# A fused recurrent attention and two mixture-of-experts layers on one core: feed-forward products for two groups of tokens at once

## The chip, the cores and the metric

The kernel runs on one core of a Trainium2 chip. The metric is the time of one execution on the device in microseconds (us), the median of repeated runs. The engines are named as in the profile: PE (TensorE, matrix products and transposes), DVE (VectorE), ACT (ScalarE), POOL (GpSimd) and SP (which here issues every load and store).

## The reference, cut to what matters

```python
# 1. attention with a decaying state: 4 batches, 8 heads, 768 steps, head size 48
for t in range(S):
    cur = einsum('bhd,bhe->bhde', u * k[t], v[t])
    y[t] = einsum('bhd,bhde->bhe', r[t], state + cur)
    state = w[t][..., None] * state + einsum('bhd,bhe->bhde', k[t], v[t])
x = y as 3072 tokens x 384
# 2. feed-forward: w_in 384 x 2048, w_out 2048 x 384 (both float64)
h = x @ w_in;  g = h * cos(h);  x = g @ w_out
# 3. soft mixture of 8 experts, 4 slots each
logits = x @ phi                                   # 3072 x 32
d = softmax of logits over the tokens;  slot_input = d.T @ x
slot_out[e] = relu(slot_input[e] @ w1[e]) @ w2[e]
out = (softmax of logits over the slots) @ slot_out
```

## The kernel before, in words

The tokens go through in pieces. Attention takes **blocks** of 128 tokens, 24 of them (j = 0 to 23); the feed-forward layer takes **groups** of 256 tokens, 12 of them (g = 0 to 11). A group needs the two blocks with its tokens.

*Attention block j.* r, k, w and v are loaded and transposed by PE (L141). DVE makes the running products of the decay by two scans over 520 columns (L156 `qt`, L164 `pt`) and scales the transposed r and k with them (L187 `L`, two halves; L199 `ks`). PE multiplies them (L208 `A`), DVE puts the causal mask on (L222, two halves), PE makes the block's part of the state (L259 `U`), DVE carries the state on (L269 `z`, L277 `st_state`), PE makes y (L288, and L297 for the term with u), and ACT and DVE store x as two parts, xh and the remainder xl (L309, L313).

*Feed-forward group g.* The hidden layer of 2048 columns is cut into 8 units of 256 (i = 0 to 7). `b_h` (L448 to L464) computes a unit in two halves of 128 hidden columns. A half takes, for each of three pieces of the 384 inputs, three products into one PSUM area: high weights times xh (L462), high weights times xl (L463), low weights times xh (L464), nine products with 256 columns (the tokens of the group). A unit's 128x512 result then goes through four steps for g = h*cos(h): a whole number of turns (`b_turns`, ACT, L474), the remainder (`b_rest`, DVE, L478), the cosine (`b_cos`, ACT, L482) and the product with h (`b_mul`, DVE, L486). PE transposes g four times (`b_t`, L494) and ACT copies that to `gt` (L499). `b_l` (L507) multiplies g with `p_sb` (w_out times phi, prepared at the start) into the group's logits. After the last unit the logits go through a running softmax over the tokens (`s_sum` to `s_dc`), and `s_e_pe` (L603) adds the weighted sum of g over the group's tokens to `E`, which DVE folds into `e_sb` (L612).

*Buffers.* x for groups 3n and 3n+1 lies in `x01`, for groups 3n+2 in a tile of its own. g has four buffers, gt twelve; h has two PSUM areas (`ps_h`), the transposed g one, the logits one, and the softmax's PSUM tiles (`ps_m`) one.

*The order.* The instructions of this part, those of SP too, are issued as the string HEAD lists them: a step per word, such as `h.2.1.0` (unit 1 of group 2, first half) or `scan.7`. Each engine executes its instructions in that order. The start of HEAD also decodes w_in and w_out from float64 (`raw`, `abs`, `mx`, `d1`, `d2a`, `d2b`, `whi`, `wn`, `wc`, `oT` and others), the word `att` closes the buffers of the attention, and then the first of the 16 expert weight tiles of 1.5 MB, `we0` to `we15`, are loaded (L678, L682): NTW of them into the space of the attention, five at `we.` words, NLATE after HEAD, the rest after the first products with experts.

*The tail.* After the last group the slot inputs, the hidden layer of the experts (`hidden`, L797) and the expert outputs (`expert_out`, L838) are computed. The outputs of the experts are columns 0 to 255 (part 0) and columns 256 to 383 (part 1); `copy_so` (L884, L885) copies each with ACT and DVE, `slots_round` (L850, L851) splits it into two, and `store` (L857 to L880) multiplies with the combine weights, copies from PSUM by ACT and DVE in turn and writes to the output: tiles 0 to 11 in two parts, tiles 12 to 23 in all 384 columns at once, 16 stores in all.

Of the kernel before, what the change touches and what calls it, by code (L numbers as in the profile page):

```python
# [21 lines left out]
def rwkv_moe_kernel(ctx: ExitStack, tc: tile.TileContext, r, k, v, w, u, w_in, w_out, phi, w1, w2, cst, out):  # L22
# [18 lines left out]
    NTW = 6  # L41
    NLATE = 3
# [9 lines left out]
    b_stack = ctx.enter_context(ExitStack())  # L52
    sm_p = b_stack.enter_context(tc.tile_pool(name="sm", bufs=2, side="right"))
# [53 lines left out]
    xh_t, xl_t = {}, {}  # L107
    x2_p = []
# [485 lines left out]
    def s_e_pe(g, hf):  # L594
# [51 lines left out]
    if True:  # L646
# [51 lines left out]
        def exp_table():  # L698
# [60 lines left out]
        with tc.manual_schedule(engines=ORDERED):  # L759
# [58 lines left out]
            crt = tw_p.tile([128, NT], F32R, tag="tw", name="cr")[0:96]  # L818
            cr = crt.rearrange("p (j b t) -> p j b t", j=4, b=NB)
# [35 lines left out]
            def store(i, tag, tiles, n):  # L855

                cols = slice(0, DM) if i is None else parts[i]  # L857
                w = cols.stop - cols.start
                if tag not in obs:
                    obs[tag] = wu_p.tile([128, 3072], F32, tag=tag, name=f"ob{tag}")  # L860
                ob = obs[tag][:, n * w:(n + len(tiles)) * w].rearrange("p (t f) -> p t f", f=w)
                nb = max(1, 512 // w)
                for b0 in range(0, len(tiles), nb):
                    k = min(nb, len(tiles) - b0)
                    ps = pb(f"o{tag}{tiles[b0]}_{w}")[:, 0:k * w].rearrange("p (t f) -> p t f", f=w)
                    for t in range(k):
                        tt = tiles[b0 + t]
                        if tt < 2 and i == 0:
# [208 lines left out]
```

## Time and profile before

| quantity | value |
|---|---|
| median of three runs | 550.89 us (550.5, 550.89, 551.18) |
| the profiled execution's own time | 552.63 us |
| its span in the profile | 550.8 us |
| mean granted TensorE clock, as a share of full speed | 0.968 |
| PE busy | 507.3 us (92% of the span), 6832 instructions |
| PE weight loads busy (beside PE's products) | 437.9 us (80%) |
| DVE busy | 433.2 us (79%), 825 instructions |
| ACT busy | 315.8 us (57%) |
| POOL busy | 124.8 us (23%) |
| chain of work that ended last | PE 64%, DVE 16%, ACT 8%, DMA 5%, SP's queue 4% |

The span is from the first to the last instruction that the profiler recorded; the profiled execution took 1.83 us more than its span, and 1.74 us more than the median. Busy times are shares over the whole span, whose stages differ: decode and first blocks, attention and feed-forward side by side, the last groups alone, the experts and the output. In a timeline, the start of an instruction is recorded; the durations of PE's products overlap, since one begins before the one ahead of it has ended.

### The profile page before, as it was taken

The page shows a single profiled execution, that of the slowest core. Times are in us where ns is not written, and L with a number is a line of the kernel's source. Part 1 is how long each engine was busy: PE and PEld are TensorE (multiplying, and loading weights), DVE is VectorE, ACT ScalarE, POOL GpSimd, SP SyncE. Part 2 cuts the span into 40 slices and gives each one's busy share as a digit, 9 for nine tenths or more (in the row PEclk, how much of TensorE's full clock was granted, in tenths as well). Part 3 has the DMA queues.
Part 4 walks back from the last instruction along what each step waited for, and adds up shares of the span by engine and source line. Part 5 has one row for each costly group of instructions (what it writes and reads, how often), then busy time and mean ns, then how long its engine had stood idle before and what let it go on. Part 6 is the DMA issues. An engine that isn't in the chain of part 4 may idle for free.

```text
span 550.8 us, 16214 instructions
## 1 busy us (share of the span) xinstructions
PE 507.3 (92%) x6832; PEld 437.9 (80%) x6832; DVE 433.2 (79%) x825; ACT 315.8 (57%) x663; POOL 124.8 (23%) x163
## 2 busy tenths in 40 slices
PE   2759879989999999999999999999999999997994
PEld 1537668879898898998988989999899899874564
DVE  4989998997888879987878898989788777563413
ACT  3246567746757465576555765656566856655422
POOL 4520120254044122321320410623124000001300
PEclk9977998999999999999999999999999999997996
DMA  8994756444432523411441243173131692477937
GB/s 195 252 247 102 177 121 182 122 75 74 73 60 44 87 50 65 74 27 28 71 72 30 52 81 56 22 126 48 20 57 30 231 377 82 175 266 275 401 116 262
DMA packets 144360, 67.52 MB, mean 123 GB/s; under 512 B 127520, under 2 KB 131616, under 8 KB 144288
## 3 DMA queue, kind: packets, MB, share of 16 engines
q1 hardware_dynamic: 144288, 66.49, 47.8%
q8 instruction: 54, 0.88, 0.7%
q14 instruction: 18, 0.15, 0.1%
HBM read 61.75 MB, written 4.72 MB: 121 GB/s over the span
## 4 chain that ended last, share of the span: by engine, by line
PE 64%; DVE 16%; ACT 8%; DMA 5%; SPq 4%; issue 2%; ACTq 0%; DVEq 0%
PE h L462 9%; PE h L464 9%; PE h L463 9%; PE gT L494 6%; PE E L603 4%; PE l L507 3%; PE y L288 3%; PE A L208 3%; PE U L259 2%; PE so L838 2%; DMA rawi<-in_moe_w_in_dram 2%; PE hps L797 2%; DVE g L478 2%; DVE L L222 2%; ACT g L482 2%
## 5 line engine op out<-in xcount | busy, mean ns | idle before, releaser
L462 PE MATMUL h<-x,wu 128*128 128x256 f32 x573 | 171.8, 300 | 1.3 <-DVE g L486 1.3
L464 PE MATMUL h<-x,wu 128*128 128x256 f32 x573 | 161.0, 281 | 0.0
L463 PE MATMUL h<-x,wu 128*128 128x256 f32 x573 | 161.0, 281 | 0.0
L462 PEld LDWEIGHTS h<-x,wu 128*128 128x128 f32 x573 | 108.9, 190 | 3.5 <-DVE g L486 1.7
L463 PEld LDWEIGHTS h<-x,wu 128*128 128x128 f32 x573 | 109.1, 190 | 0.2
L464 PEld LDWEIGHTS h<-x,wu 128*128 128x128 f32 x573 | 108.7, 190 | 0.0
L482 ACT ACTIVATE g<-g,half_pi 128x512 f32<-128x512 f32 (+1 forms) x97 | 69.4, 719 | 42.6 <-DVE g L478 41.6
L486 DVE TENSOR_TENSOR g<-g,h 128x512 f32<-128x512 f32 x96 | 64.9, 678 | 27.8 <-ACT g L482 27.2
L474 ACT ACTIVATE g<-h 128x512 int32<-128x512 f32 x96 | 57.0, 596 | 40.0 <-PE h L464 33.0
L478 DVE SCALAR_TENSOR_TENSOR g<-g,h 128x512 f32<-128x512 int32 x96 | 65.0, 678 | 17.0 <-ACT g L474 15.8
L251 POOL TENSOR_TENSOR bv<-vz,bo 64x384 f32<-64x384 f32 x48 | 43.8, 912 | 140.5 <-DVE bo L243 54.4
L499 ACT COPY gt<-gT 128x512 f32<-128x512 f32 x92 | 53.4, 584 | 31.2 <-PE gT L494 30.6
L494 PE MATMUL gT<-cs,g 128*128 128x128 f32 x384 | 58.6, 277 | 0.2
L494 PEld LDWEIGHTS gT<-cs,g 128*128 128x128 f32 x384 | 44.1, 141 | 6.0 <-issue 3.3
L169 POOL TENSOR_TENSOR ru<-rn,u_b 128x384 f32<-128x384 f32 x24 | 26.8, 1118 | 58.5 <-issue 19.5
L193 POOL MEMSET L<- 64x512 f32 x32 | 16.7, 521 | 95.9 <-PE y L288 81.5
L156 DVE TENSOR_TENSOR_SCAN qt<-wf,one_b 128x520 f32<-128x520 f32 x24 | 31.1, 1297 | 7.3 <-ACT wf L151 7.3
L222 DVE TENSOR_TENSOR L<-A,cs 64x512 f32<-64x512 f32 x48 | 33.1, 689 | 3.5 <-PE A L208 2.4
L274 ACT COPY rzs<-z 64x192 f32<-64x192 f32 x96 | 33.4, 348 | 3.6 <-DVE z L269 2.6
L187 DVE TENSOR_TENSOR L<-rT,pt 64x512 f32<-64x512 f32 x48 | 32.9, 686 | 1.6 <-PE rT L141 0.6
L164 DVE TENSOR_TENSOR_SCAN pt<-wf,ini_f 128x520 f32<-128x520 f32 x24 | 31.7, 1321 | 0.1
L288 PEld LDWEIGHTS y<-L,rzs 128*32 128x32 f32 x1536 | 25.0, 112 | 6.6 <-ACT rzs L274 2.3
(176 smaller groups left out, 845.4 us busy)
## 6 DMA issues: line engine op xcount, KB each, us to landing
we<-in_moe_w_dram SPq DMA_DIRECT2D x16, 1536.0 KB, 10.4
rawi<-in_moe_w_in_dram SPq DMA_DIRECT2D x7, 768.0 KB, 5.5
wn<-in_w_dram SPq DMA_DIRECT2D x24, 192.0 KB, 4.0
kn<-in_k_dram SPq DMA_DIRECT2D x24, 192.0 KB, 3.8
rn<-in_r_dram SPq DMA_DIRECT2D x24, 192.0 KB, 4.0
vz<-in_v_dram SPq DMA_DIRECT2D x48, 96.0 KB, 3.1
rzs<-in_v_dram SPq DMA_DIRECT2D x96, 48.0 KB, 2.8
rawo<-in_moe_w_out_dram SPq DMA_DIRECT2D x2, 1536.0 KB, 8.2
```

The source lines that it names most:

```text
L222: nc.vector.tensor_tensor(out=L[h, a], in0=ps[h], in1=mask[h].unsqueeze(1).to_broadcast([64, NS, C]), op=ALU.mult)
L251: nc.gpsimd.tensor_tensor(out=bv[h], in0=vn_t[j][h, :, c, :], in1=bo[h].to_broadcast([64, H, D]), op=ALU.mult)
L288: nc.tensor.matmul(ps[m:m + 32, o, c * C:(c + 1) * C], lhsT=rz[:, c, p, a, 32 * b:32 * b + 32], rhs=L[:, a, 2 * p + c, :], start=m not in ...
L462: nc.tensor.matmul(hp, lhsT=wh, rhs=xh[:, c, :], start=(c == 0), stop=False)
L463: nc.tensor.matmul(hp, lhsT=wh, rhs=xl[:, c, :], start=False, stop=False)
L464: nc.tensor.matmul(hp, lhsT=wl, rhs=xh[:, c, :], start=False, stop=(c == KD - 1))
L474: nc.scalar.activation(gt.bitcast(I32), hp, AF.Copy, bias=0.25, scale=1.0 / TWO_PI)
L478: nc.vector.scalar_tensor_tensor(out=gt, in0=gt.bitcast(I32), scalar=-TWO_PI, in1=hp, op0=ALU.mult, op1=ALU.add)
L482: nc.scalar.activation(gt, gt, AF.Sin, bias=half_pi[:, 0:1])
L486: nc.vector.tensor_tensor(out=gt, in0=gt, in1=hp, op=ALU.mult)
L494: nc.tensor.transpose(ps[:, tt, mm, :], gt[:, mm, tt * 128:(tt + 1) * 128], ident)
L499: (nc.vector.tensor_copy if NBK * g + i >= ATT and i in (1, 2) else nc.scalar.copy)(t, pend.pop(("gT", g, i)))
```

## The change

`WIDE_G = (2, 4, 6, 8)` names the groups that begin a pair: 2 and 3, 4 and 5, 6 and 7, 8 and 9. For these eight groups `b_h2` takes the place of `b_h`: one half of 128 hidden columns for both groups of the pair, nine products with 512 columns, 16 units (i = 0 to 15) for a pair. `b_turns`, `b_rest`, `b_cos`, `b_mul`, `b_t` and `b_tc` work on tiles of the same 128x512 as before, with the second half of the tile now the second group in place of the second half of the hidden columns. x of a pair lies in one tile, `x01` for pairs 0, 4 and 8, a tile of the `x2` pool for the others. g and gt of the wide units get one and four extra buffers. `b_l` issues four products of 512 columns for four units of a pair, and the softmax chain of each group reads its half of that PSUM tile. `s_e_pe` has pieces of 128 columns for the wide groups, 32 products a group in place of 16 of 256. `bv` has one buffer in place of two. The copy of `gt` is DVE's for the last group alone. NTW goes from 6 to 5, NLATE from 3 to 4. At the end every output tile is made in part 0 and part 1 (19 stores), each part of `so` is copied by one engine, and `expert_out(1, 0)` stands ahead of the first outputs. HEAD is a list of its own from the first word on.

Cut to the functions and lines that the text speaks of:

```diff
-    NTW = 6
-    NLATE = 3
+    NTW = 5
+    NLATE = 4
+    WIDE_G = (2, 4, 6, 8)
...
-        bv = aw.tile([128, H, D], F32, tag="bv", name=f"bv{j}")
+        bv = aw.tile([128, H, D], F32, tag="bv", name=f"bv{j}", bufs=1)
...
-            x = x01[:, g % 3] if g % 3 < 2 else x2_p[0].tile([128, 2, KD, G], F32R, tag="x", name=f"x{g}")
+            if g // 2 % 2 == 0:
+                xp = x01
+            else:
+                if g % 2 == 0:
+                    x2_t.append(x2_p[0].tile([128, 2, 2, KD, G], F32R, tag="x", name=f"x{g}"))
+                xp = x2_t[-1]
+            x = xp[:, g % 2]
...
+    def b_h2(g, i):
+
+        hp = ps_h.tile([128, 2, G], F32, tag="h", name=f"h{g}_{i}")
+        h_t[g, i] = [None, None, hp]
+        o, wt, xp = (i % 4) * 128, wu[i // 4], xp_t[g]
+        for c in range(KD):
+            wh, wl = wt[:, 0, c, o:o + 128], wt[:, 1, c, o:o + 128]
+            nc.tensor.matmul(hp, lhsT=wh, rhs=xp[:, :, 0, c, :], start=(c == 0), stop=False)
+            nc.tensor.matmul(hp, lhsT=wh, rhs=xp[:, :, 1, c, :], start=False, stop=False)
+            nc.tensor.matmul(hp, lhsT=wl, rhs=xp[:, :, 0, c, :], start=False, stop=(c == KD - 1))
...
+            pool, tag = (gx_p[1], "g5") if g in WIDE_G and i % 5 == 4 else (g_p, "g")
...
+        pool, tag = (gx_p[0], "gx") if g in WIDE_G and i % 4 == 3 else (gt_p, "gt")
+        t = pool.tile([128, 2, G], F32, tag=tag, name=f"gt{g}_{i}")
+        (nc.vector.tensor_copy if g == NG - 1 and i in (1, 2) else nc.scalar.copy)(t, pend.pop(("gT", g, i)))
...
+        if g in WIDE_G:
+            if i == 3:
+                lps_t[g] = ps_l.tile([128, 512], F32, tag="l", name=f"l{g}")
+            for m in range(i - 3, i + 1):
+                nc.tensor.matmul(lps_t[g][32 * (m % 4):32 * (m % 4) + 32, :], lhsT=p_sb[:, m, :], rhs=g_t[g, m].rearrange("p m t -> p (m t)"),
+                                 start=(m < 4), stop=(m >= MF - 4))
+            return
...
+        g0 = g // 2 * 2
+        if g0 in WIDE_G:
+            for mm in range(2):
+                for tt in range(2):
+                    for q in range(4):
+                        c = hf * 256 + mm * 128
+                        nc.tensor.matmul(ps[32 * q:32 * q + 32, c:c + 128], lhsT=dt_[:, tt, :],
+                                         rhs=gt_t[g0, 8 * hf + 2 * q + mm][:, g - g0, tt * 128:(tt + 1) * 128], start=(tt == 0), stop=(tt == 1))
+            return
...
+            def outputs(i, n0, tile_=None):
+
+                cols = parts[i]
+                n = cols.stop - cols.start
+                nt = 512 // n
...
+                if tile_ is not None and n0:
+                    nc.vector.tensor_copy(ob, ps)
+                    if t1 < nt:
+                        return
+                    ob, t0 = obs[i][:, n0 % 6], 0
+                else:
+                    (nc.vector.tensor_copy if n0 % 2 else nc.scalar.copy)(ob, ps)
+                nc.sync.dma_start(out[(n0 * nt + t0) * 128:(n0 * nt + t1) * 128, cols].rearrange("(t p) f -> p t f", p=128), ob)
...
-            copy_so(0)
-            store(0, "wu0", [0], 0)
+            nc.scalar.copy(so[:, parts[0]], ops[0][:, 0:256])
+            expert_out(1, 0)
+            outputs(0, 0, 0)
             slots_out(0)
...
-lw.0 wT.0 wf.0 scan.0 z.0.0 raw.i.2 abs.i.2 mx.i.2 d1.i.2 sr.0 d2a.i.2 d2b.i.2 lk.0 kT.0 sp.0 raw.i.0.0 abs.i.0.0 mx.i.0.0 lr.0
+raw.i.0.0 abs.i.0.0 mx.i.0.0 raw.i.0.1 d1.i.0.0 abs.i.0.1 lr.0 z.0.0 d2a.i.0.0 mx.i.0.1 d1.i.0.1 d2a.i.0.1 d2b.i.0.0 d2b.i.0.1
```

Three places of the order follow. In the names, `h_4`, `g_0` and the like are feed-forward tiles by unit; the last number is an instruction's tile.

PE, in group 2, around the first half of its logits; before:

```order
L464 MATMUL h_4_2273<-x_1629,wu_698 128x256
L259 MATMUL U_2327<-vz_123,ksn_2309 64x96 x8
L288 MATMUL y_2338<-L_1942,rzs_126 32x64 x32
L507 MATMUL l_2373<-g_0_2158,p_sb 32x256 x2
L507 MATMUL l_2373<-g_1_2113,p_sb 32x256 x2
L507 MATMUL l_2373<-g_2_2299,p_sb 32x256 x2
L507 MATMUL l_2373<-g_3_2176,p_sb 32x256 x2
L494 MATMUL gT_0_2395<-cs,g_0_2158 128x128 x4
L462 MATMUL h_5_2409<-x_1629,wu_698 128x256
```

These rows end with the next half of a unit. In the change the same place has groups 2 and 3 together (L484 and L482 are products of `h`, L530 logits, L515 transposes of g, L210 `A`, L290 and L299 y, L143 and L217 transposes of the attention):

```order
L484 MATMUL h_8_2740<-x_1583,wu_691 128x512
L210 MATMUL A_2750<-L_2629,ks_2725 64x64 x16
L530 MATMUL l_2488<-g_4_2451,p_sb 32x512
L530 MATMUL l_2488<-g_5_2650,p_sb 32x512
L530 MATMUL l_2488<-g_6_2520,p_sb 32x512
L530 MATMUL l_2488<-g_7_2525,p_sb 32x512
L290 MATMUL y_2774<-L_2395,rzs_125 32x64 x32
L143 MATMUL rT_2807<-cs,rn_117 128x128 x4
L299 MATMUL y_2774<-cs,bv_2812 128x128 x3
L515 MATMUL gT_5_2836<-cs,g_5_2650 128x128 x4
L217 MATMUL kN_2843<-cs,ks_2725 128x128 x4
L482 MATMUL h_11_2848<-x_1583,wu_691 128x512
```

Before, pairs of products with 256 columns make the logits of units 0 to 3 of group 2, and the halves of units come in 256 columns; in the change four products with 512 columns make the logits of units 4 to 7 for both groups, and each product of `h` has 512 columns.

DVE, where the first instructions for group 2 stand (names with `g2_`); before:

```order
L156 SCALAR_TENSOR_TENSOR qt8_2026<-wf_127,one_b_128 128x520
L478 SCALAR_TENSOR_TENSOR g1_7_2028<-g1_7_2028,h1_7_1923 128x512
L486 TENSOR_TENSOR g1_7_2028<-g1_7_2028,h1_7_1923 128x512
L160 RECIPROCAL ini_f_129<-qt8_2026 128x8
L164 SCALAR_TENSOR_TENSOR pt8_2044<-wf_127,ini_f_129 128x520
L616 COPY e_sb_110<-E0_1971 128x512
L617 COPY st_s_113<-sg0_1786 128x1
L313 TENSOR_TENSOR x01_115<-y6_1990,x01_115 128x3x128
L222 TENSOR_TENSOR L7_1942<-A7_1945,cs_103 64x512 x2
L478 SCALAR_TENSOR_TENSOR g2_1_2113<-g2_1_2113,h2_1_2070 128x512
L486 TENSOR_TENSOR g2_1_2113<-g2_1_2113,h2_1_2070 128x512
L199 TENSOR_TENSOR ks8_2161<-kT8_2089,qt8_2026 128x512
```

Around the remainder and product of unit 1 of group 2 (L478, L486) stand scan, `L`, mask and `ks` of blocks 7 and 8. The same place in the change (there L499 is the remainder, L507 the product, L189 `L`, L224 the mask, L201 `ks`, L271 `z`, L166 `pt`):

```order
L189 TENSOR_TENSOR L8_2145<-rT8_2130,pt8_2082 64x512 x2
L507 TENSOR_TENSOR g1_7_2000<-g1_7_2000,h1_7_1981 128x512
L322 TENSOR_TENSOR x2_1583<-y7_2097,x2_1583 128x3x128
L499 SCALAR_TENSOR_TENSOR g1_6_2205<-g1_6_2205,h1_6_2068 128x512
L507 TENSOR_TENSOR g1_6_2205<-g1_6_2205,h1_6_2068 128x512
L224 TENSOR_TENSOR L8_2145<-A8_2181,cs_103 64x512 x2
L201 TENSOR_TENSOR ks9_2222<-kT9_2200,qt9_2136 128x512
L279 TENSOR_TENSOR st_state_130<-U8_2169,z8_0_2138 128x192
L271 TENSOR_TENSOR z8_1_2225<-st_state_130,qt8_1949 128x192
L499 SCALAR_TENSOR_TENSOR g2_0_2242<-g2_0_2242,h2_0_2210 128x512
L166 SCALAR_TENSOR_TENSOR pt9_2246<-wf_127,ini_f_129 128x520
L507 TENSOR_TENSOR g2_0_2242<-g2_0_2242,h2_0_2210 128x512
```

Here it is blocks 8 and 9: the attention is about one block further when group 2 begins.

SP, the loads of expert weights from the last one of `att` on; before:

```order
L678 DMA we5_6930<-in_moe2_w1_dram 128x3x1024
L678 DMA we6_7355<-in_moe2_w1_dram 128x3x1024
L682 DMA we10_7357<-in_moe2_w2_dram 128x4x768
L678 DMA we7_7406<-in_moe2_w1_dram 128x3x1024
L682 DMA we8_7408<-in_moe2_w2_dram 128x4x768
L682 DMA we9_7421<-in_moe2_w2_dram 128x4x768
L682 DMA we11_7453<-in_moe2_w2_dram 128x4x768
L682 DMA we12_7455<-in_moe2_w2_dram 128x4x768
L682 DMA we13_7457<-in_moe2_w2_dram 128x4x768
L682 DMA we14_7565<-in_moe2_w2_dram 128x4x768
L682 DMA we15_7579<-in_moe2_w2_dram 128x4x768
```

Five loads (`we11` to `we15`) stand behind `we9`. In the change, from `we4`, the last one of `att`:

```order
L717 DMA we4_6438<-in_moe2_w1_dram 128x3x1024
L717 DMA we5_6679<-in_moe2_w1_dram 128x3x1024
L717 DMA we6_6831<-in_moe2_w1_dram 128x3x1024
L721 DMA we9_6904<-in_moe2_w2_dram 128x4x768
L717 DMA we7_6918<-in_moe2_w1_dram 128x3x1024
L721 DMA we8_6920<-in_moe2_w2_dram 128x4x768
L721 DMA we10_6942<-in_moe2_w2_dram 128x4x768
L721 DMA we11_6944<-in_moe2_w2_dram 128x4x768
L721 DMA we12_6946<-in_moe2_w2_dram 128x4x768
L721 DMA we13_6948<-in_moe2_w2_dram 128x4x768
L721 DMA we14_7056<-in_moe2_w2_dram 128x4x768
L721 DMA we15_7070<-in_moe2_w2_dram 128x4x768
```

Six loads (`we10` to `we15`) stand behind `we8`; `we5` comes by a word of its own and `we9` ahead of `we7`.

## Rows read from the trace of the kernel before

**Rows 1.** The page's busy time of each engine and its chain that ended last.

```profile
PE 507.3 (92%) x6832; PEld 437.9 (80%) x6832; DVE 433.2 (79%) x825; ACT 315.8 (57%) x663; POOL 124.8 (23%) x163
...
PE 64%; DVE 16%; ACT 8%; DMA 5%; SPq 4%; issue 2%; ACTq 0%; DVEq 0%
```

**Rows 2.** Stretches: us, busy PE, PEld, DVE, ACT, POOL, then PE's clock, DMA share, GB/s.

```profile
50.00:125.00 75.00, 66.95 (x855) 55.59 (x854) 71.07 (x110) 46.13 (x92) 16.61 (x15) 0.98 0.56 130
125.00:475.00 350.00, 346.81 (x4852) 314.58 (x4852) 290.67 (x576) 216.96 (x457) 84.89 (x104) 1.00 0.35 76
```

**Rows 3.** PE's timeline along stretches of products: start us, us, engine, line.

```profile
230.68 0.60 PE L494 MATMUL gT<-cs,g 128*128 128x128 f32 x4
231.03 0.37 PE L462 MATMUL h<-x,wu 128*128 128x256 f32 x1
231.24 0.28 PE L463 MATMUL h<-x,wu 128*128 128x256 f32 x1
...
232.39 0.28 PE L463 MATMUL h<-x,wu 128*128 128x256 f32 x1
...
234.31 0.28 PE L464 MATMUL h<-x,wu 128*128 128x256 f32 x1
```

**Rows 4.** PE's timeline where products of 256 and of 512 columns stand together.

```profile
87.59 0.60 PE L404 MATMUL wl<-ai,cs 128*128 128x256 f32 x2
87.83 0.47 PE L405 MATMUL wl<-wu,neg 128*128 128x256 f32 x1
88.14 1.02 PE L404 MATMUL wl<-ai,cs 128*128 128x512 f32 x2
88.60 0.79 PE L405 MATMUL wl<-wu,neg 128*128 128x512 f32 x1
```

**Rows 5.** PE's timeline in the tail, products with 32 weight columns.

```profile
522.70 6.25 PE L838 MATMUL so<-we,wo_sb 128*32 128x256 f32 x112
...
531.16 1.08 PE L838 MATMUL so<-we,wo_sb 128*32 128x128 f32 x32
```

**Rows 6.** DVE's groups by line: count, busy us, mean ns, idle before.

```profile
L222 DVE TENSOR_TENSOR L<-A,cs 64x512 f32<-64x512 f32 x48 | 33.1, 689 | 3.5 <-PE A L208 2.4
L187 DVE TENSOR_TENSOR L<-rT,pt 64x512 f32<-64x512 f32 x48 | 32.9, 686 | 1.6 <-PE rT L141 0.6
L164 DVE TENSOR_TENSOR_SCAN pt<-wf,ini_f 128x520 f32<-128x520 f32 x24 | 31.7, 1321 | 0.1
L156 DVE TENSOR_TENSOR_SCAN qt<-wf,one_b 128x520 f32<-128x520 f32 x24 | 31.1, 1297 | 7.3 <-ACT wf L151 7.3
L269 DVE TENSOR_TENSOR z<-st_state,qt 128x192 f32<-128x192 f32 x44 | 17.8, 404 | 1.0
...
L199 DVE TENSOR_TENSOR ks<-kT,qt 128x512 f32<-128x512 f32 x24 | 16.4, 682 | 1.5 <-PE kT L141 1.1
```

**Rows 7.** PE's steps of the attention in the chain that ended last: start us, us.

```profile
234.59 1.08 PE A L208 x32
235.67 0.66 PE U L259 x16
```

**Rows 8.** What DVE waited for: us in total, times, longest us.

```profile
DVE g L486 <- ACT g L482: 27.8, 40, 1.5
DVE g L478 <- ACT g L474: 16.7, 24, 2.2
```

**Rows 9.** The stretch of the last expert loads, and SP's timeline there.

```profile
503.00:526.00 23.00, 22.88 (x374) 13.83 (x370) 9.49 (x27) 7.93 (x21) 5.87 (x9) 0.94 0.91 344
...
502.94 10.54 SPq L682 DMA_DIRECT2D we<-in_moe_w_dram  x5
```

**Rows 10.** Bytes by the page, the last stretch, and ACT's first copy of expert outputs.

```profile
HBM read 61.75 MB, written 4.72 MB: 121 GB/s over the span
...
538.50:550.80 12.30, 5.54 (x24) 5.38 (x24) 4.28 (x8) 3.23 (x7) 0.00 (x0) 0.56 0.79 275
...
529.02 0.27 ACT L884 COPY wo_sb<-so 128x128 f32<-128x128 f32 x1 [5.74 <-PE so L838]
```

More of the change, by code (lines that the diff above doesn't have):

```diff
@@ L853, in rwkv_moe_kernel @@
             obs = {}
[L855 to L868, printed above, removed]
-                            nc.tensor.matmul(ps[:, t], lhsT=cf[:, tt * 128:(tt + 1) * 128], rhs=so[:, cols], start=True, stop=True)
-                        elif i is None:
-                            o = tiles[0] * 128 + b0 + t
-                            nc.tensor.matmul(ps[:, t], lhsT=crt[:, o:o + 255:2], rhs=sr[:, cols], start=True, stop=True)
-                        else:
-                            nc.tensor.matmul(ps[:, t], lhsT=crt[:, tt * 128:(tt + 1) * 128], rhs=sr[:, cols], start=True, stop=True)
-                    pend["ob"] = 1 - pend.get("ob", 0)
-                    (nc.scalar.copy if pend["ob"] else nc.vector.tensor_copy)(ob[:, b0:b0 + k], ps)
-                t0 = tiles[0] * 128
-                dst = out[t0:t0 + len(tiles) * 128, cols]
-                nc.sync.dma_start(dst.rearrange("(p t) f -> p t f" if i is None else "(t p) f -> p t f", p=128), ob)
@@ L940 @@
-close h.1.0.0 gT.0.6 oT.12 pc.2 pT.2 oc.12 lr.6 gc.0.6 scan.6 h.1.0.1 ru.6 mul.0.7 sr.6 ps.2 bo.6 oT.14 oT.15 oc.14 l.0.5 oc.15
-om.3 kT.6 turns.1.0 rest.1.0 rz.4.0 h.1.1.0 gT.0.7 ks.6 pc.3 pT.3 ps.3 z.5.0 st.5.0 z.5.1 st.5.1 cos.1.0 mul.1.0 y.4 l.0.7 rT.6
-h.1.1.1 h.1.2.0 lw.7 ru.5 bo.5 sp.6 wT.7 h.1.2.1 L.6 lz.5 turns.1.1 rz.5.1 gc.0.7 rest.1.1 lv.6 lr.8 rz.5.0 sum.0 cos.1.1 yb.4
-xh.4 turns.1.2 xl.4 rest.1.2 wf.7 bv.5 mul.1.1 gT.1.0 cos.1.2 mul.1.2 gc.1.0 scan.7 y.5 A.6 lc.0 mask.6 h.1.3.0 h.1.3.1 turns.1.3
@@ L1024 @@
[L1024 to L1026 removed]
+            for n0 in range(6):
+                outputs(1, n0)
+HEAD = """
+raw.i.0.0 abs.i.0.0 mx.i.0.0 raw.i.0.1 d1.i.0.0 abs.i.0.1 lr.0 z.0.0 d2a.i.0.0 mx.i.0.1 d1.i.0.1 d2a.i.0.1 d2b.i.0.0 d2b.i.0.1
@@ new lines @@
+oT.12 turns.0.7 ps.2 oc.13 d2b.o.7 close oT.14 gT.0.5 oc.14 rest.0.7 oT.15 oc.15 U.5 l.0.5 oc.12 cos.0.7 om.3 scan.6 bo.5 z.5.0
+mul.0.7 rz.5.0 st.5.0 pc.3 z.5.1 A.5 mask.5 lv.6 pT.3 rz.5.1 ps.3 turns.1.1 rest.1.1 gc.0.5 sr.6 sp.6 h.1.0.0 h.1.0.1 wT.7 wf.7
+turns.1.0 cos.1.1 l.0.7 y.4 yb.4 xh.4 sum.0 rest.1.0 cos.1.0 gT.0.7 mul.1.1 scan.7 mul.1.0 kT.6 xl.4 st.5.1 ks.6 gc.0.7 h.1.3.0
+h.1.3.1 turns.1.3 rest.1.3 cos.1.3 gT.1.1 rT.6 lc.0 gc.1.1 h.1.2.0 kN.6 h.1.2.1 gT.1.0 ru.6 lr.8 turns.1.2 ksn.6 bv.5 lz.6 bo.6
@@ new lines @@
+wT.9 gT.1.3 kN.8 ksn.8 gc.1.3 cos.1.7 E.0.0 E.0.1 lz.7 mul.1.4 gT.1.4 h.1.6.0 lv.8 rz.7.0 sp.8 ru.9 zl.9 wf.9 rz.7.1 l.1.5 y.7
+rT.8 lr.10 scan.9 z.8.0 sr.9 es.0 gc.1.4 zl.8 gT.1.5 bo.9 gc.1.5 yb.7 h.1.6.1 U.8 L.8 mul.1.7 A.8 xh.7 xl.7 kT.9 turns.1.6
+rest.1.6 cos.1.6 mul.1.6 h2.2.0 mask.8 ks.9 st.8.0 z.8.1 rT.9 gT.1.7 kN.9 turns.2.0 rest.2.0 cos.2.0 sp.9 mul.2.0 lw.11 lz.8 lw.10
+h2.2.1 ksn.9 L.9 gc.1.7 rz.8.1 l.1.7 rz.8.0 sum.1 turns.2.1 lk.10 y.8 st.8.1 rest.2.1 cos.2.1 mul.2.1 wT.10 gT.1.6 wf.10 bv.8
```

267 lines of the change are left out of this document (131 added, 136 removed).

## The prediction

> **What bounds the kernel now.** I read the page's totals first, then the busy times by stretch, then PE's timeline, the waits of DVE and the chain of waits. PE is busy for 507.3 of 550.8 us and makes 64% of the chain, DVE 433.2 us and 16% [rows 1]. The totals hide two stages. From 50 to 125 us DVE is busy for 71.07 of 75 us and PE for 66.95; from 125 to 475 us PE is busy for 346.81 of 350 and DVE for 290.67 [rows 2]. So DVE sets the pace while the weights are decoded and the first blocks go through, and PE sets it in the long stage behind. A change is worth there what it takes off the bounding engine: DVE's work ahead of about 125 us, PE's work behind it, and at the end the chain from the last group to the last store.
>
> **The change part by part.** The sum is made against the profiled execution, 552.63 us (a span of 550.8 and 1.83 around it); the median of the runs is 550.89, or 1.74 lower, and I carry the difference over to it unchanged.
>
> *Products of 512 columns.* Counted in the order of PE, the feed-forward products of groups 2 to 9 go from 1152 with 256 columns to 576 with 512. The number of columns streamed is the same, so the gain is only what each instruction costs beyond its columns. In an unbroken stretch sixteen spacings, from 232.39 to 234.31 us, take 1.92 us, 0.120 each; I take 0.119, since the times are read to 0.01, so two products take 0.238 [rows 3]. The nearest products with 512 columns are those of L404: two of them take 88.60 - 88.14 = 0.46 us, 0.23 each, where two of 256 take 87.83 - 87.59 = 0.24 [rows 4]. The difference is 0.008 us, 576 x 0.008 = 4.6 us less. The trace's steps of 0.01 us leave this open: between 0 (a product of 512 takes exactly two of 256) and 7 us (0.012 each). 576 weight loads go as well; they lie beside the products in this stretch, and I give them nothing more.
>
> *Fewer starts of a stretch.* Uninterrupted stretches of `h` products go from 135 to 107 and those of logits from 38 to 28. The first product after the four transposes of g has its successor 0.21 us later (231.03 to 231.24) where 0.12 is usual [rows 3], so 38 x 0.09 = 3.4 us less. Since not each start shows this, the bounds are 1 and 5 us.
>
> *Expert sums in pieces of 128 columns.* `E` has 32 products of 128 columns for a wide group in place of 16 of 256, 128 products more in all, the columns the same. Thirty-two of 128 columns took 1.08 us and 112 of 256 took 6.25 us, or 16 in 0.89 [rows 5]; but each row includes the run-out of its last product, which weighs more in the short one. I take a third of the difference, 0.06 us a group, +0.5 in all, with 0 and 0.19 x 8 = 1.5 as bounds.
>
> *The attention runs further ahead.* The wide products need x of two groups, so four blocks where two did, and the list does their work earlier. Counted to the first remainder of group 2, DVE has 237 instructions instead of 219. In five groups of rows these are one `qt` scan more, two masks, two `L`, two `ks`, and four `z`: 1.297 + 2 x 0.689 + 2 x 0.686 + 2 x 0.682 + 4 x 0.404 = 7.0 us [rows 6]. Seven shorter ones (state, `bo`, x and a reciprocal) are estimated with `z`'s 0.404, another 2.8. In the same stretch of the list PE gets one more `A` at 1.08, two more `U` at 0.66 [rows 7] and six more transposes of four at 0.35 (from 230.68 to 231.03, [rows 3]), 4.5 us, and some y. DVE is the bound up to here [rows 2], so the stage grows by 9.8; PE, with 5 of them to do that it need not do later, gets back only that. I take +4.5 net. The bounds are 0 (DVE has gaps ahead of it: 17 and 28 us of waits for ACT in the span, [rows 8], which the extra work can fill) and 9.8 (PE does nothing in that time that helps it later).
>
> *Expert weights.* NTW falls to 5, so `we5` waits for a feed-forward buffer, and behind the last groups six loads stand in SP's queue where five did. From 503 to 526 us the DMA engines were 91% busy at 344 GB/s, with the last five loads issued from 502.94 us on [rows 9]: 23 us for five, 4.6 each. A sixth ends near 530.6 us. The eight experts' products for part 0 end near 529.0, where ACT's copy begins, and the last 16 of them take 112-fold 6.25 / 7 = 0.89 [rows 5, 10], so they begin near 528.1 and would be 2.5 us late. I take +2.4, with 0 (buffers come free earlier) and 4.6 (the whole load) as bounds. What is queued behind on SP is only the stores, which come later anyway.
>
> *Output.* Before, 12.30 us at 275 GB/s, 3.4 of the 4.72 MB written, are moved in the last stretch, from 538.5 us on [rows 10], since tiles 12 to 23 wait for part 1. In the change part 0 of all tiles, two thirds of the bytes, goes out before that; 1.6 MB stay behind part 1, 1.8 MB less, which is 6.6 us of transfer. The copies out of PSUM and their chain are as long as before (18 of 512 columns), and `so` part 0 is copied whole by ACT, where ACT took 0.27 us for its half [rows 10]; so I take a third, -2, with -4 and +2 (three more stores, one engine's longer copy) as bounds.
>
> *At nothing.* The single `bv` buffer makes POOL wait for the y term (POOL is busy for 124.8 us of the span, [rows 1] less than a quarter, so the work queued behind such a wait has room; without that room PE's y would wait for it). The copies of `gt` for group 10 go from DVE to ACT, the less busy of the two in every stretch read [rows 2]. The new beginning of the list decodes `raw.i.0` first; the same DVE instructions follow in another order, and the bound by DVE is unchanged.
>
> *Sum.* -4.6 - 3.4 + 0.5 + 4.5 + 2.4 - 2 = -2.6 us: 552.63 - 2.6 = 550.0 for a profiled execution, 550.89 - 2.6 = **548.3** for the median. Its own range is 545 to 550: the small terms against each other.
>
> **The rivals.**
> *DVE takes over in the wide stage (slower).* Two groups' remainders and products come close together, and at the first product of group 6 the list is further ahead still: two `qt` scans, two `pt` scans, eight halves of `L` and mask, one `ks`, three `z`, 2 x 1.297 + 2 x 1.321 + 8 x 0.688 + 0.682 + 3 x 0.404 = 12.6 us of DVE's work [rows 6], against some 3 us of PE's. For it: in the 350 us DVE is at 83% as it stands [rows 2], and its `L486` waits only 28 us for ACT [rows 8], so it has little room. Against it: 59 us of DVE's stage are idle. It decides if DVE is busy throughout up to group 6. Then the lead costs 12.6 - 3 = 9.6 instead of 4.5, +5.1: 553.4.
> *512 columns cost just twice 256, or nearly.* Rows 4 are only two pairs, read to 0.01 us. If the spacing were columns at the clock and a small constant, the gain of the first part shrinks. At a gain of 1.4 us the sum is +0.6, 551.5; at none +2.0, 552.9. The Trainium skill, "TensorE: Matmul & The Clock Gate", section "Back-to-back issue gap", gives for an isolated gap the columns at 2.4 GHz plus about 2.5 ns: by it 576 fewer products save 1.4 us. By it 256 columns take 0.109 us and 512 take 0.216; the rows have 0.119 and 0.23, about 0.01 more for either, so the trace supports its shape and leaves its constant open.
> *Stalls at the change of pairs (slower).* Two softmax chains now follow one another through the one `ps_m` buffer, and the logits of the last four units wait for the last `b_mul`. A wait for ACT of up to 2.2 us is in the trace [rows 8]; once a pair, 4 x 2.2 = 8.8: 557.1. Against it: the next pair's first units stand between.
> *The lead is free and the weights are on time (faster).* If the gaps of DVE take the lead, and buffers come free early, 4.5 and 2.4 go away: -9.5, 541.4. For it: 27.8 and 16.7 us of waits [rows 8]. Against it: 95% DVE in the stage where the lead is built up [rows 2].
>
> **How the numbers follow.** Forecast 0.37; DVE takes over 0.27; 512 columns no cheaper 0.13; stalls 0.08; free lead 0.15. The predicted time is the forecast's, 548.3. What a measurement of this kernel can tell from no change is about 0.2%, 1.1 us. Faster by more: most of the forecast (0.33) and the free lead (0.15), 0.48. Within it: the forecast's edge (0.04), the mild ends of the first and second rival (0.04 and 0.07), 0.15. Slower: the rest, 0.37. The range goes from 542.5, which takes in most of the way to the free lead, to 555.5, which takes in the first rival with its bounds and leaves out the stalls.
>
> **What would show it.** The spacing of two `h` products with 512 columns: 0.230 us if the first term is right, 0.238 if not. In the stretch where groups 2 and 3 are begun PE should stand idle for some 4 or 5 us, waiting for DVE, and not in groups 6 to 9; idle time of PE there by L507 or L499 of DVE would be the first rival. `so` products should wait for a DMA by about 2 us near the end, and the last store should end some 20 us after the first copy of `so`, where it was 21.8. The prediction is wrong if PE is idle at the start of each pair, or if the stage up to group 2 is not longer than before.

## The result, and the profile after

The changed kernel takes 557.22 us (median of six runs, 554.78 to 560.29) against 551.0 us: 1.0113 of the kernel before, with a 95% interval of 1.0088 to 1.0137. It is 6.2 us slower; 548.3 was forecast, and the range ended at 555.5. The profiled execution of the change is one of its fastest (555.35 us, a span of 553.4), so the two profiles differ by less than the medians do.

The page of the change, busy times and chain (against [rows 1]):

```profile
PE 503.8 (91%) x6402; PEld 404.8 (73%) x6402; DVE 435.4 (79%) x821; ACT 314.9 (57%) x663; POOL 131.0 (24%) x163
...
PE 54%; DVE 30%; ACT 7%; DMA 5%; issue 4%; SPq 0%; ACTq 0%; DVEq 0%
```

PE has 430 instructions less, but is busy for only 3.5 us less. DVE's share of the chain has gone from 16% to 30%.

The two stages again, by busy time (columns as in [rows 2]), and PE's two longest waits in the first:

```profile
50.00:125.00 75.00, 65.06 (x859) 53.78 (x858) 72.09 (x109) 49.04 (x100) 19.24 (x16) 1.00 0.52 120
125.00:475.00 350.00, 344.38 (x4375) 280.84 (x4378) 289.08 (x571) 210.49 (x446) 86.43 (x102) 1.00 0.34 64
...
PE wl L413 <- DVE L L224: 2.2, 1, 2.2
PE y L290 <- DVE L L189: 1.9, 1, 1.9
```

The longest one there before:

```profile
PE U L259 <- DMA vz<-in_v_dram: 2.4, 1, 2.4
```

PE does 1.9 us less in the first stage and 2.4 less in the second than before, so it stands idle for that much more in each; DVE is busy for 1.0 us more in the first. In the first stage two waits of PE for DVE's `L` and mask make 4.1 us; before, the longest wait there was one for a load of v.

The end is read best from PE's timeline: the sum after the last `E`, the part 0 products with expert weights, and the first output (against [rows 5, 9, 10]):

```profile
503.44 0.38 PE L805 MATMUL sum<-st_s,cs 128*128 128x1 f32 x2
...
521.74 4.52 PE L877 MATMUL so<-we,wo_sb 128*32 128x256 f32 x80
526.99 1.07 PE L877 MATMUL so<-we,wo_sb 128*32 128x256 f32 x16 [0.73 <-DMA we<-in_moe_w_dram]
531.00 2.79 PE L877 MATMUL so<-we,wo_sb 128*32 128x256 f32 x32 [2.94 <-DMA we<-in_moe_w_dram]
533.72 0.70 PE L908 MATMUL o<-wo_sb 128*128 128x256 f32 x2
...
531.00:536.00 5.00, 5.00 (x43) 3.32 (x44) 0.67 (x2) 1.48 (x4) 0.00 (x0) 0.72 0.05 18
```

The last line is a stretch of five us (columns as in [rows 2]). Before, the same sum and the first output product:

```profile
504.47 0.59 PE L765 MATMUL sum<-st_s,cs 128*128 128x1 f32 x2
...
529.66 0.70 PE L870 MATMUL owu<-wo_sb 128*128 128x256 f32 x2 [0.71 <-DVE wo_sb L885]
```

So up to the last group the change is 1.0 us ahead, and at the first output 4.1 us behind. In between, PE waits for the expert weights twice, 3.7 us in all, and runs more slowly behind the waits: the row at 531.00 has 32 products, 16 of part 0 and the first 16 of part 1, and from 531 to 536 us the granted clock is 0.72. From the first output product to the end of the span it takes 553.4 - 533.72 = 19.7 us, where it took 550.8 - 529.66 = 21.1. The 1.0 us of lead should not be built on: the profile of the kernel before is of one of its longer executions, and in `tail_new` and `before_six` below, whose order up to there is the old one, the sum began at 502.49 and 502.69, earlier than in the change.

### The profile page after: what moved, and what is told of

Read it like the earlier page. It is cut to its first block, busy times and chain, and to the rows that moved or that the text cites. A ratio compares the mean times of both kernels' runs of the same rounds, so it can differ in the third digit from the quotient of the medians.

```text
span 553.4 us, 15345 instructions
## 1 busy us (share of the span) xinstructions
PE 503.8 (91%) x6402; PEld 404.8 (73%) x6402; DVE 435.4 (79%) x821; ACT 314.9 (57%) x663; POOL 131.0 (24%) x163
## 4 chain that ended last, share of the span: by engine, by line
PE 54%; DVE 30%; ACT 7%; DMA 5%; issue 4%; SPq 0%; ACTq 0%; DVEq 0%
PE h L482 6%; PE h L484 6%; PE h L483 6%; PE gT L515 5%; DMA we<-in_moe_w_dram 3%; DVE g L499 3%; DVE g L507 3%; PE l L530 3%; DVE L L189 3%; PE A L210 3%; DVE L L224 2%; DVE pt L166 2%; PE y L290 2%; ACT g L503 2%; PE U L261 2%
## 5 line engine op out<-in xcount | busy, mean ns | idle before, releaser
L507 DVE TENSOR_TENSOR g<-g,h 128x512 f32<-128x512 f32 x96 | 65.0, 679 | 30.6 <-ACT g L503 30.0
L253 POOL TENSOR_TENSOR bv<-vz,bo 64x384 f32<-64x384 f32 x48 | 47.9, 998 | 165.5 <-PE y L299 54.4
L499 DVE SCALAR_TENSOR_TENSOR g<-g,h 128x512 f32<-128x512 int32 x96 | 64.9, 677 | 22.5 <-ACT g L495 21.8
L482 PE MATMUL h<-x,wu 128*128 128x512 f32 x192 | 81.2, 423 | 1.4 <-DVE g L507 1.4
L484 PE MATMUL h<-x,wu 128*128 128x512 f32 x192 | 75.8, 395 | 0.0
L483 PE MATMUL h<-x,wu 128*128 128x512 f32 x192 | 75.6, 394 | 0.0
L515 PE MATMUL gT<-cs,g 128*128 128x128 f32 x384 | 58.6, 276 | 0.1
L471 PE MATMUL h<-x,wu 128*128 128x256 f32 x189 | 57.0, 301 | 1.0 <-DVE g L507 0.9
L472 PE MATMUL h<-x,wu 128*128 128x256 f32 x189 | 53.4, 283 | 0.0
L515 PEld LDWEIGHTS gT<-cs,g 128*128 128x128 f32 x384 | 44.2, 141 | 12.5 <-issue 3.9
L473 PE MATMUL h<-x,wu 128*128 128x256 f32 x189 | 53.3, 282 | 0.0
L482 PEld LDWEIGHTS h<-x,wu 128*128 128x128 f32 x192 | 36.1, 188 | 9.4 <-DVE g L507 3.3
L484 PEld LDWEIGHTS h<-x,wu 128*128 128x128 f32 x192 | 36.0, 188 | 8.5
L483 PEld LDWEIGHTS h<-x,wu 128*128 128x128 f32 x192 | 36.2, 189 | 6.0
L471 PEld LDWEIGHTS h<-x,wu 128*128 128x128 f32 x189 | 36.3, 192 | 1.9 <-DVE g L507 1.7
L472 PEld LDWEIGHTS h<-x,wu 128*128 128x128 f32 x189 | 36.4, 193 | 0.1
L473 PEld LDWEIGHTS h<-x,wu 128*128 128x128 f32 x189 | 36.2, 192 | 0.0
```

Of the source, the lines that this page charges most:

```text
L471: nc.tensor.matmul(hp, lhsT=wh, rhs=xh[:, c, :], start=(c == 0), stop=False)
L472: nc.tensor.matmul(hp, lhsT=wh, rhs=xl[:, c, :], start=False, stop=False)
L473: nc.tensor.matmul(hp, lhsT=wl, rhs=xh[:, c, :], start=False, stop=(c == KD - 1))
L482: nc.tensor.matmul(hp, lhsT=wh, rhs=xp[:, :, 0, c, :], start=(c == 0), stop=False)
L483: nc.tensor.matmul(hp, lhsT=wh, rhs=xp[:, :, 1, c, :], start=False, stop=False)
L484: nc.tensor.matmul(hp, lhsT=wl, rhs=xp[:, :, 0, c, :], start=False, stop=(c == KD - 1))
```

## Experiments

The theories: the loss is made at the end by six loads behind one another (the prediction's fifth term, too small); or by DVE's lead where the wide stage begins (its fourth term, or its first rival); beside these, what the wide products, the output part and other steps of the list are worth. Ratios are to the kernel before, measured beside each group of runs, with 95% intervals; a difference of two ratios is open by both intervals.

### The yardstick, and the change's output part alone

`after_again` is the changed kernel once more.

> The changed kernel once more, as the yardstick of this group of runs on this chip: about 1.011 of the kernel before, if the first comparison holds. Its profile should again show waits of some 3 to 4 us of the part 0 expert products for the last expert loads (0.73 and 2.94 us in the first profile), if these belong to the order of the loads and not to one execution.

1.011 (1.0075 to 1.0146), a median of 556.78 us, with waits of 0.87 and 2.85 us at the same place. PE's clock falls behind them, and in this execution for longer: the granted clock in five us from 526, 531 and 536 us was 1.00, 0.56 and 0.75 (columns as in [rows 2]):

```profile
526.00:531.00 5.00, 2.80 (x48) 1.20 (x40) 0.00 (x0) 0.00 (x0) 0.00 (x0) 1.00 0.92 353
531.00:536.00 5.00, 3.49 (x34) 2.05 (x35) 0.00 (x0) 0.37 (x1) 0.00 (x0) 0.56 0.03 13
536.00:541.00 5.00, 5.00 (x57) 4.14 (x58) 1.96 (x4) 2.19 (x5) 0.00 (x0) 0.75 0.23 75
```

`tail_new` is the kernel before with this in place of `store` and `copy_so`:

```diff
-            copy_so(0)
-            store(0, "wu0", [0], 0)
+            nc.scalar.copy(so[:, parts[0]], ops[0][:, 0:256])
+            expert_out(1, 0)
+            outputs(0, 0, 0)
...
```

> The kernel before with the changed output part alone (all tiles in two column parts, each part of the expert outputs copied by one engine, expert_out(1, 0) ahead of the first outputs). In the two profiles the time from the end of the part 0 expert products to the end of the span is 21.85 us before and 19.6 us in the change. If the output part is worth that by itself: 2.2 us faster, 0.996 of before. If the shorter end in the change only comes from its late expert weights (outputs wait for nothing else by then): no difference, 1.000.

0.9963 (0.9947 to 0.998): 2.0 us faster. The output part is a gain by itself, of the size forecast.

### One load fewer, part 0 columns first, and six loads in the kernel before

`five_late` leaves one of the six loads out (expert 2 is then computed with expert 1's weights, and the number of products stays):

```diff
-        for i in range(NLATE):
-            load_e(NTW + 5 + i, late_a if i == 0 else late_b, "late")
+        wt[NTW + 5] = wt[NTW + 4]
+        for i in range(1, NLATE):
+            load_e(NTW + 5 + i, late_b, "late")
```

> The changed kernel with one of the six expert loads behind the last group left out (the tile of expert 2's second weights is the one of expert 1, so the sums of expert 2 are computed with expert 1's weights); the number of products is the same. If six loads in place of five set the end of the expert products: the last load lands 4.5 us earlier, the waits of 0.73 and 2.94 us go, PE's clock does not fall behind them, and the time is 4 to 5 us less than the changed kernel. If the loss is made earlier, by the lead of the attention's work in DVE, and the weights are late in this one execution only: 0 to 1 us.

0.9986 (0.9967 to 1.0005), some 6.8 us off the changed kernel, more than was expected. The 128 products that had stood in three pieces go through at once:

```profile
521.40 6.69 PE L878 MATMUL so<-we,wo_sb 128*32 128x256 f32 x128
```

`cols_first` has all products and all weights, and only loads in another order:

```diff
+                if idx >= SPLIT:
+                    load_cols(t, idx, slice(0, 256))
...
+                if e == 2:
+                    for idx in range(SPLIT, 2 * NE):
+                        load_cols(wt[idx], idx, slice(256, DM))
```

> The changed kernel with the last four expert weight tiles loaded in two pieces: of experts 4 to 7 first the columns of part 0 (256 of 384), then, behind the products of expert 2's hidden layer in SP's list, the columns of part 1. All products are as in the change. If the part 0 products wait because six whole loads go through the DMA engines one behind another at their full rate: a third of four loads, 6 us of transfer, moves behind the point where it hurts, the waits of 0.7 and 2.9 us go, and the time is that of the run with one load fewer, 5 to 6.5 us less than the changed kernel. If the loads are late because their buffers come free late: still late, 0 to 2 us less.

0.999 (0.9963 to 1.0017). The waits are gone:

```profile
521.66 6.92 PE L890 MATMUL so<-we,wo_sb 128*32 128x256 f32 x128
```

From 1.0113 and 1.011 to 0.999 it gains some 6.7 us, a little more than the whole loss.

`before_six` puts the six loads into the kernel before:

```diff
-    NTW = 6
-    NLATE = 3
+    NTW = 5
+    NLATE = 4
...
```

> The kernel before with five places for expert weights in the space of the attention and four behind the groups, and nothing else changed: six loads behind the last group instead of five. If the order of the loads alone makes the loss at the end: waits of 2 to 3.5 us of the part 0 products, PE's clock down behind them, and 5 to 7 us more than before, 1.009 to 1.013. If the loss needs the changed list as well (attention's buffers are free 20 us later there): under 2 us more.

1.0102 (1.0064 to 1.0139), 556.3 us: as slow as the changed kernel, from these two numbers alone (the five `we.` words of the list count one lower with them).

```profile
502.69 0.38 PE L765 MATMUL sum<-st_s,cs 128*128 128x1 f32 x2
...
520.42 4.52 PE L838 MATMUL so<-we,wo_sb 128*32 128x256 f32 x80
525.40 1.07 PE L838 MATMUL so<-we,wo_sb 128*32 128x256 f32 x16 [0.46 <-DMA we<-in_moe_w_dram]
529.32 1.93 PE L838 MATMUL so<-we,wo_sb 128*32 128x256 f32 x16 [2.85 <-DMA we<-in_moe_w_dram]
...
531.00:536.00 5.00, 4.29 (x34) 2.84 (x34) 1.14 (x3) 1.01 (x3) 0.00 (x0) 0.50 0.08 28
```

Sixteen products at full clock took 1.07 us with their run-out; behind the wait they took 1.93, and the granted clock stood at 0.50 from 531 to 536 us. So the price, 5.6 us by the ratio, is the waits of 3.3 us and some 2.3 more, which fit the slower work behind them. It lies behind the groups: from the start of the sum to the end of the span it takes 550.8 - 504.47 = 46.3 us before, 555.0 - 502.69 = 52.3 here, 50.0 in the change and 45.0 in `cols_first`. The loads into the attention's space, which start at 464.3 us in the change and at 439.9 before, are not needed for it.

### What products of 512 columns are worth

`split256` computes a wide unit in two halves:

```diff
-        for c in range(KD):
...
+        for t in range(2):
+            for c in range(KD):
+                wh, wl = wt[:, 0, c, o:o + 128], wt[:, 1, c, o:o + 128]
+                nc.tensor.matmul(hp[:, t], lhsT=wh, rhs=xp[:, t, 0, c, :], start=(c == 0), stop=False)
...
```

> The changed kernel with each wide unit computed as two times nine products of 256 columns, in the same order of steps, so that stretches begin as rarely as in the change. If the products of 512 columns are worth 0.008 us against two of 256 (the prediction's first term by itself): 4.6 us slower than the changed kernel. If the column stream alone sets the time: no difference in PE's work. If what the change gained on these products came from the rarer starts of a stretch: under 1 us slower.

1.0107 (1.0057 to 1.0157), like the changed kernel; with an interval of some 2.8 us either way its time says little, and the products' own times decide. Taken from each product's start to the next one's start or its own end, all wide products took 140.9 us in the change and 142.0 here: 1.2 us for 576 pairs, 0.002 each instead of 0.008. Two places of one stretch each, the change's at 512 columns and this run's at 256:

```profile
355.23 0.39 PE L483 MATMUL h<-x,wu 128*128 128x512 f32 x1
...
358.96 0.39 PE L484 MATMUL h<-x,wu 128*128 128x512 f32 x1
```

```profile
354.82 0.28 PE L483 MATMUL h<-x,wu 128*128 128x256 f32 x1
...
358.10 0.28 PE L485 MATMUL h<-x,wu 128*128 128x256 f32 x1
360.84 0.28 PE L485 MATMUL h<-x,wu 128*128 128x256 f32 x1
...
362.61 0.28 PE L485 MATMUL h<-x,wu 128*128 128x256 f32 x1
```

Sixteen spacings at 512 take 3.73 us, 0.233 each; twenty-nine at 256 take 3.28 us, 0.113 each, and fifteen a little later 1.77, 0.118. The kernel before had 0.120 in one stretch [rows 3]. The differences between stretches of one width are larger than what the width brings.

### The lead of DVE, and the beginning of the list

`lw_first` (on `cols_first`) begins the list as before:

```diff
-raw.i.0.0 abs.i.0.0 mx.i.0.0 raw.i.0.1 d1.i.0.0 abs.i.0.1 lr.0 z.0.0 d2a.i.0.0
...
+lw.0 wT.0 wf.0 scan.0 raw.i.0.0 abs.i.0.0 mx.i.0.0 raw.i.0.1 d1.i.0.0 abs.i.0.1 lr.0 z.0.0 d2a.i.0.0
...
```

> The run with part 0 columns first, and the list beginning as before: load, transposes and scan of the first block's decay ahead of the first weights. If the new beginning costs time (PE's first product comes at 8.7 us of the span where it came at 4.6): up to 4 us less than without it. If the beginning is worth nothing, as the prediction has it, since DVE sets the pace there and its work is only reordered: 0, within 1 us.

0.9995 (0.9973 to 1.0016): no difference.

`pad_early` (on `five_late`) adds DVE work at six places:

```diff
+        def pad():
+            nc.vector.tensor_tensor(out=one_b, in0=one_b, in1=one_b, op=ALU.mult)
...
-rest.2.0 cos.2.0
+pad rest.2.0 cos.2.0
...
```

> The run with one of six late loads left out, and six more DVE products of 128x521 elements (one_b by itself, about 0.7 us each, 4 us in all) spread from the scan of block 8 to the first units of groups 2 and 3, where the changed list has the attention further ahead. If DVE's lead work is on the path there (the prediction's term of 4.5 us): 3 to 4 us more than without them. If PE sets the pace and DVE has room: 0 to 1 us.

1.0022 (1.0001 to 1.0044) against 0.9986: 2.0 us for six products of 0.69 us, 4.2 in all. Between the two theories: about half of DVE's work there shows in the time, with some 1.6 us of the 2.0 open by the intervals.

`mask_off` (on `five_late`) takes DVE work away from there:

```diff
-h2.2.0 mask.8 ks.9
+h2.2.0 mc.8 mp.8 ks.9
...
```

> The run with one of six late loads left out, and the masks of blocks 8 and 9 made by a copy of ACT and a product of POOL in place of DVE's two products each: 2.8 us of DVE's work less just where groups 2 and 3 begin. If the lead of DVE's work costs time there: 1.5 to 3 us less than without it. If not: 0, or a little more, since the mask takes longer by that way.

0.9996 (0.9967 to 1.0025), no gain. The waits of PE from 125 to 200 us tell why it doesn't decide. First with DVE's mask (`five_late`), then without (`mask_off`):

```profile
PE h L482 <- DVE g L507: 1.2, 3, 0.8
PE h L471 <- DVE g L507: 0.9, 1, 0.9
PE A L210 <- DVE L L189: 0.7, 1, 0.7
```

```profile
PE y L290 <- POOL L L236: 2.2, 2, 1.3
PE A L210 <- DVE L L189: 0.6, 1, 0.6
...
PE h L482 <- DVE g L507: 0.2, 1, 0.2
```

The waits for DVE's g went from 2.1 to 0.2 us, and 2.2 us of waits for POOL's mask came in their place.

`mxp_wide` and `mxp_narrow` relieve DVE ahead of group 2, on `no_tab` and `tail_no_tab` (below):

```diff
-mx.o.4
+mxp.o.4
...
```

> The changed kernel with part 0 columns first and without the table step, and with six of the decode's maxima (w_in parts 5 and 7, w_out parts 4 to 7) moved from DVE to POOL: 6 x about 0.57 = 3.4 us less of DVE's work ahead of group 2, where DVE is busy for 72.1 of 75 us. If the stage up to group 2 is longer by DVE's extra work (the prediction's lead of 4.5 us): 2 to 3 us less than without the move, and at least 1 us more gain than the same move has in the kernel before. If DVE's work is not what bounds there: 0, or slower, since POOL takes longer for it.

> The kernel before with the new output part and without the table step, with the same six maxima moved from DVE to POOL. DVE is busy for 70.8 of 75 us in that stage here too. If DVE bounds the stage as read from the profile: 1 to 3 us less, and the fastest version. If the decode's chain bounds it, in which POOL is the slower member: 0 or slower.

1.0153 (1.0131 to 1.0176) and 0.9997 (0.9982 to 1.0012), against 0.9977 and 0.9938 without: 9.7 and 3.2 us slower. The relief failed, since POOL takes 2.1 to 2.4 us for one where DVE takes 0.56:

```profile
L366 POOL TENSOR_SCALAR ao<-ao 128x768 f32<-128x768 f32 x4 | 9.5, 2384 | 18.4 <-ACT ao L362 18.4
```

In these two runs the delay costs the changed list three times as much as the list before. That the old list's steps leave more room is one reading, and DVE waits for POOL there for 7.5 us in `mxp_wide` and 2.6 in `mxp_narrow`; but PE's clock has a part in it. In `mxp_wide` it falls behind a wait, as at the end of the changed kernel; the third row is `mxp_narrow`:

```profile
93.11 1.93 PE L290 MATMUL y<-L,rzs 128*32 128x64 f32 x64 [2.90 <-DVE L L189]
90.00:100.00 10.00, 7.10 (x125) 6.38 (x124) 9.49 (x13) 3.13 (x5) 3.38 (x3) 0.66 0.56 132
90.00:100.00 10.00, 7.80 (x154) 6.66 (x153) 9.29 (x15) 5.11 (x10) 6.29 (x6) 1.00 0.45 113
```

From 50 to 125 us the granted clock was 0.90 in `mxp_wide` and 1.00 in `mxp_narrow`. How much of the difference is the clock, and how much the order, these runs do not separate.

### A step that the prediction passed over: ACT's table

The step `tab` (a one-element exponential) stood in group 9 before and stands in group 2 in the change. In both it is followed by two more table loads. ACT's loads before, then in the change (start us, us):

```profile
430.79 1.28 ACT L699 ACT_TABLE_LOAD   x1
433.28 1.28 ACT L482 ACT_TABLE_LOAD   x1
436.40 1.28 ACT L630 ACT_TABLE_LOAD   x1
```

```profile
178.47 1.28 ACT L739 ACT_TABLE_LOAD   x1
180.94 1.28 ACT L503 ACT_TABLE_LOAD   x1
183.72 1.28 ACT L586 ACT_TABLE_LOAD   x1
```

`no_tab` (on `cols_first`), `tab_back` (there, behind `dc.8`) and `tail_no_tab` (on `tail_new`) move or remove the word:

```diff
-z.10.0 tab lc.1
+z.10.0 lc.1
```

> The run with part 0 columns first, without the step that makes ACT load its table for the exponential (a one-element activation). Before, that step stood in group 9; in the change it stands in group 2, and in either profile it brings three table loads of 1.28 us one behind another, the exponential's, then those of the cosine and of the softmax again, while the table at the end is loaded anew anyway. If these loads in group 2 hold up the chain ACT, DVE, PE where the wide stage begins (waits of 1.8 us of DVE and 0.3 and 0.8 us of PE in that place): 1 to 3 us less than with the step. If DVE's lead work or nothing bounds there: 0.

> The run with part 0 columns first, with that step moved to where it stood before, behind the copy of the softmax weights of group 8. If only the place of the table loads matters: as without the step, or up to 1 us more, if it matters there too; if the loads cost nothing anywhere: as the run with part 0 columns first.

> The kernel before with the new output part alone, without the table step. If the three loads in group 9 are hidden behind PE there, as its profile has it (PE is busy throughout from 425 to 475 us): as with the step, 0.996 of before. If they cost something there too: up to 2 us less, 0.993, and this would be the fastest of all versions.

`no_tab` took 0.9977 (0.9956 to 0.9997), 0.7 us less than with the step, with intervals that overlap. `tab_back` took 1.0046 (1.0023 to 1.0068), 3.1 us more, which neither expectation had: in the changed list the old place is a worse one. There PE was busy for 70.47 us from 400 to 475 us, and for 73.40 in `cols_first`. `tail_no_tab` took 0.9938 (0.9915 to 0.9961), 546.54 us: 1.4 us less than `tail_new`, and **the lowest time of all versions**, 10.7 us below the changed kernel, though its interval overlaps that of `tail_new`. That the loads of group 9 are hidden behind PE, as its busy time suggests, is then neither shown nor refuted.

## Why the prediction was wrong, point by point

- **Expert weights: the term that was mis-sized.** +2.4 us was forecast, with 4.6 as the bound; the loss is 5.6 us in `before_six` and 6.7 from `cols_first`. The mechanism was right: five loads became six, and the last was forecast to land near 530.6 us; the products that need it began at 531.00. Two things were missed. The need was taken from the time before, one wait only, where there were two (0.73 and 2.94 us). And the cost was ended with the wait: PE's granted clock, 1.00 ahead of it, fell to 0.50 to 0.72 for the five us behind it, so the work behind took up to 1.8 times as long (1.93 us for 1.07). My bound, one whole load, was no bound. At 0.50 TensorE stands at 1.2 GHz instead of 2.4. The Trainium skill, "TensorE: Matmul & The Clock Gate", section "What's actually happening", names these two states and idleness as what leads to the lower one; the runs here agree, with the 0.50 of `before_six` right behind a wait.
- **Products of 512 columns: wrong.** -4.6 us was forecast; 1.2 us was measured, near the second rival's 1.4. Two pairs read to 0.01 us carried the term. The time itself, though, did not come out at that rival's 551.5. The 1.4 was an estimate from the constant in the Trainium skill, "TensorE: Matmul & The Clock Gate", section "Back-to-back issue gap"; the saving agrees with it, while the spacings themselves, 0.113 to 0.120 and 0.233 us, lie above the 0.109 and 0.216 of that rule.
- **Fewer starts: near in size, the cause shown in part.** All feed-forward products took 218.2 us before and 213.7 in the change, by the same sum as above; 4.4 less, of which 1.2 are the width. Some 3.2 are left, forecast 3.4. But the trace has 117 unbroken stretches of `h` before and 96 in the change, 21 fewer where 28 were counted, and the logits, from which ten more starts were to come, took 25.2 and 25.3 us. At 0.09 the starts of `h` make 1.9; the rest would be the spacing inside the stretches, which varies as shown above. That the total came so near is in part luck.
- **Expert sums: small, and the sign is open.** By the same sum the products of `E` took 23.6 us before and 22.5 in the change, 1.1 less, where +0.5 was forecast. Over all runs this sum goes from 22.9 to 23.6 with the old pieces and from 22.5 to 24.1 with the new ones, so no sign is shown.
- **The lead of DVE: a longer stage, as forecast; its net cost too small and only half explained.** The 288th product of `h`, two groups' worth, starts 10.4 us later in the change (first row) than before:

```profile
158.59 0.28 PE L473 MATMUL h<-x,wu 128*128 128x256 f32 x1
148.21 0.28 PE L464 MATMUL h<-x,wu 128*128 128x256 f32 x1
```

  Most of that is won back by the last group. With the loads on time (`cols_first`) the changed list is 0.0027 of 551 us, 1.5 us, slower than the kernel before with the same output part, though the last three points make PE's work some 5.5 us shorter (1.2, 3.2 and, as far as it holds, 1.1). So about 7 us, with some 2 either way, are lost in what else the list changes, within the bounds of 0 to 9.8 and above the 4.5 that was taken. The two longest waits ahead of 125 us are for DVE, as forecast, and from 125 to 200 us, where groups 2 and 3 begin, PE waits 2.9 us for DVE (0.4 before), where 4 or 5 were to show. Work added to DVE costs about half its time. Work taken away from DVE moved the wait to POOL. How much of the 7 us is DVE's lead, and how much anything else in the new list, stays open.
- **The first rival (DVE takes over up to group 6): no.** From 200 to 475 us PE's waits for DVE's products are as short as before (0.3 us, 0.5 before), and DVE is no busier from 125 to 475 us.
- **Stalls at the change of pairs: no.** The waits for the softmax steps are 2.0 us in all in the profile of the change from 125 to 475 us (1.3 ahead of `E`, 0.7 ahead of the logits' `lc`), not 8.8.
- **Output: right.** -2 was forecast and 2.0 measured.
- **At nothing.** The beginning of the list is worth nothing, as said. The moved `tab` was not seen at all. The single `bv` buffer makes POOL wait for the y term, as said:

```profile
L253 POOL TENSOR_TENSOR bv<-vz,bo 64x384 f32<-64x384 f32 x48 | 47.9, 998 | 165.5 <-PE y L299 54.4
```

  What that costs PE no run tests; it is one candidate for the open 7 us, as are the copies of `gt` that went to ACT.

So the sum -1.2 - 3.2 - 1.1 + 7.0 + 6.7 - 2.0 gives the +6.2 that was measured; it closes because the seven is what the other terms leave over, not a measurement of its own. Of the distance from the forecast, the expert weights make 4.3 us (6.7 for 2.4), the products of 512 columns 3.4 and the lead 2.5; the sums of `E`, as measured, take 1.6 back.

## What to carry to other kernels

Where a transfer's end sets the next step, ask for the time of need and of landing after the change, and price what an idle TensorE does to the work behind the wait too: here a wait of 3.3 us cost 5.6. Loading the columns that are needed first removed it without a byte more of memory. And when a whole list of steps is new, look for the steps whose cost is not in their own length, such as a table load that brings two others.

## What was not expected of the hardware

The spacing of products with 256 columns is not one number: 0.113 us and 0.118 us in two stretches 6 us apart of one execution, 0.120 in the kernel before, at a granted clock of 1.00 in all three. One step to ACT's exponential table brings three loads of 1.28 us, since the cosine and then the softmax load theirs anew; in `no_tab` all three are gone, though what they cost in time is not settled.
